# First q phase: the last column tile of q reads inputs with their shift already added

## The chip, the cores and the metric

One core of one Trainium2 chip. The metric is the device time of one execution in microseconds (us), median of several runs. The granted clock of the tensor engine was 1.00.

A ratio of two kernels is the mean time of one kernel's fast runs over the mean of the other's fast runs of the same rounds, so it is not quite the ratio of the medians quoted beside it.

Engines: PE is the tensor engine, PEld its weight loads, DVE the vector engine, ACT the scalar engine, POOL the third elementwise engine, SP the engine that issues DMA. A "tile" of x is 128 tokens, a "chunk" four tiles (512 tokens), a "k-tile" 128 of the 1024 features of a chunk. The "warm-up" is the matmuls at the kernel's start whose results nobody uses; a "pair" is one weight load with its matmul. A DMA "lands" when its data have arrived. "Lost time" is time that PE stands still where it could have run on.

## The reference, cut to what matters

```python
mod = (_silu(c) @ w_mod).reshape(c.shape[0], 6, 1, -1)
sa, ca, ga, sb, cb, gb = ...                       # six rows of 1024
h = _layernorm(x) * (1 + ca) + sa                  # x is 2048 x 1024
qkv = h @ wqkv                                     # q: the first 1024 columns
phi = lambda t: jnp.where(t > 0, t + 1, jnp.exp(t)) + 1e-06
pq, pk = phi(q), phi(k)
# ... linear attention, output projection, second norm, SwiGLU: not touched here
```

The shift `sa` is known later than the scale `1 + ca`, because its weights are loaded later. The kernel therefore starts q on inputs that are scaled but not shifted, and adds what is missing as a bias: q = Wq^T (scaled) + Wq^T sa.

## The kernel before

`P.pe`, `P.dve`, `P.act`, `P.pool` append an instruction to an engine's list; semaphores are worked out from the addresses that instructions touch. For PSUM this helper's unit is a whole bank: an access by another engine waits for the last one of this bank. HT[:, 0] holds the first chunk, transposed, in eight k-tiles dt; MODCOL holds the scale and shift columns.

```python
def h0_shift(dt):       # adds the shift to a scaled k-tile, in place
    P.dve("tensor_scalar", out=HT[:, 0, dt, :], in0=HT[:, 0, dt, :], scalar1=MODCOL[:, 1, dt:dt + 1],
          scalar2=None, op0=ALU.add)

def bias_mm(dts):       # column nt of bank 0 += Wq[dt, nt]^T sa[dt]: a matmul of one column
    for nt in range(NDT):
        for dt in dts:
            P.pe("matmul", out=PS[:, 0, 16 + nt:17 + nt], lhsT=WQK[:, dt, nt * 128:(nt + 1) * 128],
                 rhs=MODTMP[:, dt:dt + 1], start=False, stop=(dt == 3), skip_group_check=True)

def bias_fin():
    P.dve("tensor_copy", out=BIASQ[:], in_=PS[:, 0, 16:24])

def q_phase_chunk0(side):
    # [cut: q column tiles 0..6 over k-tiles 0..5; the scale columns; k-tiles 6, 7 get scale and shift at once]
    mod_sc(WSA, 0, range(4, 6))          # PE: sa for k-tiles 4, 5
    fin_sa(4, 2, True)                   # DVE: copy it to MODTMP and MODCOL
    for nt in range(7):
        if nt == 2:
            bias_mm((4, 5))
        q_part(nt, qb[nt], (6,))
    for nt in range(7):
        if nt == 1:
            mod_sc(WSA, 0, range(4))     # PE: sa for k-tiles 0..3
            fin_sa(0, 4, True)
            ln_ops[1][0]()               # DVE: statistics of tile 5 (second chunk), two halves
            ln_ops[1][1]()
        if nt == 4:
            bias_mm(range(4))
            bias_fin()
        q_part(nt, qb[nt], (7,))
    ln_ops[1][2]()
    ln1_rstd1(5)                         # DVE, then POOL: 1/std of tile 5
    for f in act_mv_ops(4):
        f()
    neg_rstd(4)                          # DVE, then POOL: 1/std of tile 4
    q_phi = lambda nt: phi_evac(..., bias=BIASQ[:, nt:nt + 1])
    for i, dt in enumerate((4, 5, 0, 1, 2, 3, 6, 7)):       # q column tile 7, in bank 0
        P.pe("matmul", out=PS[:, 0, :], lhsT=WQK[:, dt, 896:1024], rhs=HT[:, 0, dt, :], start=(i == 0),
             stop=(i == 7))
    for dt in (4, 5):
        h0_shift(dt)                     # k of this chunk needs shifted tiles
    ln1_xn(5); th_dma(5)                 # DVE: normalize tile 5; SP: its DMA transpose
    for dt in range(4):
        h0_shift(dt)
    ln1_xn(4); th_dma(4)
    for nt in range(8):
        q_phi(nt)                        # ACT and DVE: evacuate q
        # side work: statistics, normalization and transposes of tiles 6 and 7
# then k of chunk 0 (8 groups of 8 matmuls), in which DVE scales and shifts chunk 1,
# then k and q of chunk 1, ... and the G products (x^T times k), which read "pk" tiles
```

## Time and profile before

| | before |
|---|---|
| median of 6 runs | 831.10 us (830.88 to 831.48) |
| span of the profiled run | 829.0 us |
| PE busy | 819.6 us, 99% |
| last matmuls of the bias products | 26.33 to 27.11 us |
| last transpose of the second chunk lands | 41.80 us |
| 16 KB instruction fetch between 30 and 60 us | at 38.54 us, 1.03 us long |

First the page of the kernel before: busy time of each engine, and the engines of the chain that ended last.

```profile
PE 819.6 (99%) x4005; PEld 379.2 (46%) x4083; DVE 312.5 (38%) x665; ACT 197.5 (24%) x336; POOL 40.4 (5%) x57
...
PE 97%; DVE 2%; issue 1%; ACT 0%; DVEq 0%; ACTq 0%
```

PE is the limit. Only work that PE does, or that PE waits for, can count.

The PE timeline of the kernel before, from the sa matmuls on. Columns: start in us, length, engine, line, operation, out<-in, shapes, count.

```profile
20.55 0.54 PE L176 MATMUL ps<-siluc,wsa 128*128 128x1 bf16 x16
...
23.18 0.55 PE L176 MATMUL ps<-modtmp,wqk 128*128 128x1 bf16 x16
23.59 1.46 PE L176 MATMUL ps<-ht,wqk 128*128 128x512 bf16 x6
...
26.33 0.94 PE L176 MATMUL ps<-modtmp,wqk 128*128 128x1 bf16 x32
27.13 23.04 PE L176 MATMUL ps<-ht,wqk 128*128 128x512 bf16 x104
```

The lines that read `modtmp` are the 48 bias products. The 32 of them run from 26.33 to the next line's start, 27.13: 0.80 us, 25 ns each. A length such as 0.94 includes the modelled end of the last one, so starts are what to subtract. After 27.13 there is not one gap.

The DVE timeline of the kernel before, in the same stretch; brackets tell how long the engine sat idle and who ended that.

```profile
25.93 0.16 DVE L176 CAST modtmp<-ps 128x4 bf16<-128x4 f32 x1 [2.81 <-PE ps L176]
26.00 0.15 DVE L176 COPY modcol<-ps 128x4 f32<-128x4 f32 x1
26.22 1.29 DVE L176 BATCH_NORM_STATS2 stats<-xres 128x6 f32<-128x512 bf16 x2
27.42 0.15 DVE L176 COPY biasq<-ps 128x8 f32<-128x8 f32 x1
...
28.23 0.61 DVE L176 TENSOR_SCALAR ht<-ht,modcol 128x512 bf16<-128x512 bf16 x2
28.75 0.54 DVE L176 TENSOR_SCALAR xres<-xres,mv,rstd 128x1024 bf16<-128x1024 bf16 x1
29.21 1.13 DVE L176 TENSOR_SCALAR ht<-ht,modcol 128x512 bf16<-128x512 bf16 x4
30.26 0.54 DVE L176 TENSOR_SCALAR xres<-xres,mv,rstd 128x1024 bf16<-128x1024 bf16 x1
...
35.92 0.99 DVE L176 TENSOR_SCALAR xres<-xres,mv,rstd 128x1024 bf16<-128x1024 bf16 x2
...
41.93 2.67 DVE L176 TENSOR_SCALAR ht<-ht,modcol 128x512 bf16<-128x512 bf16 x8 [1.25 <-DMA ht<-xres]
```

Six shifts at 28.23 and 29.21, four normalizations at 28.75, 30.26 and 35.92 (`xres<-xres,mv,rstd`), and at 41.93 the scaling of the second chunk, which waits for its DMA transposes.

The PEld timeline of the kernel before at that place: the first k group of the second chunk.

```profile
42.89 1.61 PEld L176 LDWEIGHTS ps<-ht,wqk 128*128 128x128 bf16 x8
44.65 0.92 PEld L176 LDWEIGHTS ps<-ht,wqk 128*128 128x128 bf16 x5 [0.16 <-DVE ht L176]
```

One weight load, at 44.65, waits for DVE. PE loses nothing yet, but it is close.

Stretches of the kernel before around the instruction fetch. Columns: stretch, its length, busy time of PE, PEld, DVE, ACT, POOL with counts, clock, DMA share, GB/s.

```profile
38.30:38.60 0.30, 0.30 (x3) 0.13 (x2) 0.30 (x2) 0.30 (x2) 0.00 (x0) 1.00 1.33 259
...
39.20:40.20 1.00, 1.00 (x6) 0.49 (x5) 1.00 (x5) 1.00 (x3) 0.00 (x0) 1.00 0.61 10
40.20:41.00 0.80, 0.80 (x6) 0.35 (x4) 0.48 (x2) 0.80 (x2) 0.00 (x0) 1.00 1.09 217
```

The last column falls to 10 GB/s for a microsecond, in the middle of the transposes that DVE waits for. The trace's packet records show what is there: one packet of 16,384 bytes in the instruction queue from 38.54 to 39.57 us, and the transposes' packets of 256 bytes thinning out after it. The run has 32 such packets for PE's 4083 weight loads and as many matmuls; so I take them for PE's instruction fetches.

### The profile page before, as it was taken

What the parts mean: (1) busy time and instruction counts of PE and PEld (TensorE: products, weight loads), DVE (VectorE), ACT (ScalarE), POOL (GpSimd) and SP (SyncE); (2) the same over time, 40 slices, a digit from 0 to 9 for tenths busy, and PEclk for the clock granted to TensorE, in tenths of its full rate; (3) what the DMA queues carried; (4) which work ended last, traced back from release to release, by engine and by line L of the source; (5) the groups of instructions that cost most, each with busy time, mean ns of one, the idle gap of its engine ahead of it and who ended that gap; (6) DMA issues with size and microseconds to landing.
All of it is one profiled execution on the core that took longest, in us unless ns stands there. A gap on an engine that the chain in (4) does not pass through costs nothing.

```text
span 829.0 us, 9939 instructions
## 1 busy us (share of the span) xinstructions
PE 819.6 (99%) x4005; PEld 379.2 (46%) x4083; DVE 312.5 (38%) x665; ACT 197.5 (24%) x336; POOL 40.4 (5%) x57
## 2 busy tenths in 40 slices
PE   8999999999999999999999999999999999999998
PEld 4544444454444444444444444444444444444444
DVE  5797986756955521121221112122111111221111
ACT  4757641323242111011111101111110111111011
POOL 1010000000130000030000003000000300000000
PEclk9999999999999999999999999999999999999999
DMA  9969655928397995700455571045557004553000
GB/s 320 291 151 232 149 155 172 202 103 304 63 255 231 292 252 153 189 25 18 123 153 154 150 184 33 18 124 153 154 150 189 26 19 123 152 154 86 0 26 26
DMA packets 199245, 119.28 MB, mean 144 GB/s; under 512 B 57880, under 2 KB 182944, under 8 KB 199200
## 3 DMA queue, kind: packets, MB, share of 16 engines
q1 hardware_dynamic: 199184, 118.65, 52.8%
q8 instruction: 32, 0.52, 0.3%
q14 instruction: 13, 0.11, 0.0%
q10 hardware_dynamic: 16, 0.00, 0.0%
HBM read 100.67 MB, written 4.33 MB: 127 GB/s over the span
## 4 chain that ended last, share of the span: by engine, by line
PE 97%; DVE 2%; issue 1%; ACT 0%; DVEq 0%; ACTq 0%
PE ps L176 97%; DVE acc L176 1%; DVE pkt L176 0%; DVE e L176 0%; DVE pqt L176 0%; DVE ht L176 0%; DVE mask L176 0%; ACT e L176 0%; DVE xres L176 0%; DVE zsel L176 0%; DVE modcol L176 0%; DVEq L247 0%; ACTq L247 0%
## 5 line engine op out<-in xcount | busy, mean ns | idle before, releaser
L176 PE MATMUL ps<-h2t,guu 128*128 128x512 bf16 x878 | 210.1, 379 | 0.9
L176 PE MATMUL ps<-h2t,gug 128*128 128x512 bf16 x878 | 209.9, 379 | 0.9
L176 DVE TENSOR_TENSOR at<-sg,ps 128x512 bf16<-128x512 bf16 x112 | 77.0, 688 | 282.7 <-PE ps L176 270.1
L176 ACT ACTIVATE sg<-ps 128x512 bf16<-128x512 f32 x112 | 67.0, 598 | 309.6 <-PE ps L176 298.2
L176 PEld LDWEIGHTS ps<-h2t,guu 128*128 128x128 bf16 x896 | 87.7, 98 | 105.7
L176 PEld LDWEIGHTS ps<-h2t,gug 128*128 128x128 bf16 x896 | 87.6, 98 | 105.5
L176 PE MATMUL ps<-wd_a,at 128*128 128x512 bf16 (+1 forms) x501 | 111.5, 377 | 0.5
L176 PE MATMUL ps<-ht,wqk 128*128 128x512 bf16 x499 | 110.5, 379 | 0.8
L176 PE MATMUL ps<-wd_b,at 128*128 128x512 bf16 (+1 forms) x378 | 84.7, 377 | 0.4
L176 PEld LDWEIGHTS ps<-wd_a,at 128*128 128x128 bf16 x512 | 50.1, 98 | 59.7
L176 DVE TENSOR_TENSOR ut<-att,gb_b 128x512 bf16<-128x512 bf16 (+1 forms) x32 | 14.3, 446 | 166.9 <-ACT att L176 166.9
L176 PEld LDWEIGHTS ps<-ht,wqk 128*128 128x128 bf16 x512 | 49.5, 98 | 58.6 <-DVE biasq L176 0.2
L176 ACT ACTIVATE att<-ps 128x512 bf16<-128x512 f32 (+1 forms) x32 | 17.4, 591 | 182.1 <-PE ps L176 182.1
L176 PEld LDWEIGHTS ps<-wd_b,at 128*128 128x128 bf16 x384 | 37.6, 98 | 44.6
L176 PE MATMUL ps<-pk,xres 128*128 128x512 bf16 x250 | 55.9, 379 | 0.4 <-issue 0.2
L176 PE MATMUL ps<-mw,pqt 128*128 128x512 bf16 x250 | 55.8, 379 | 0.3
L176 POOL TENSOR_SCALAR h2t<-h2t,modcol 128x512 bf16<-128x512 bf16 x32 | 26.5, 844 | 383.0 <-DMA h2t<-xn 383.0
L176 ACT ACTIVATE e<-ps 128x512 bf16<-128x512 f32 x56 | 33.2, 604 | 31.7 <-PE ps L176 20.4
L176 PEld LDWEIGHTS ps<-mw,pqt 128*128 128x128 bf16 x256 | 24.8, 98 | 30.2 <-DVE xres L176 0.4
L176 PEld LDWEIGHTS ps<-pk,xres 128*128 128x128 bf16 x256 | 24.9, 98 | 29.9 <-issue 0.4
L176 ACT ACTIVATE junk<-xres 128x1024 bf16<-128x1024 bf16 x24 | 25.4, 1058 | 35.1 <-DVE xres L176 34.9
L176 DVE SCALAR_TENSOR_TENSOR xres<-ps,xres 128x512 bf16<-128x512 f32 x32 | 21.4, 688 | 12.3 <-PE ps L176 11.5
(107 smaller groups left out, 346.3 us busy)
## 6 DMA issues: line engine op xcount, KB each, us to landing
gug<-in_B_w_gate_dram SPq DMA_DIRECT2D x56, 512.0 KB, 4.1
guu<-in_B_w_up_dram SPq DMA_DIRECT2D x56, 512.0 KB, 5.3
xres<-in_A_x_dram SPq DMA_DIRECT2D x20, 256.0 KB, 7.8
rb<-recip_den SPq DMA_DIRECT2D x8, 512.0 KB, 12.0
stgx<-in_w_mod_dram SPq DMA_DIRECT2D x2, 2048.0 KB, 8.2
wd_a<-in_B_w_down_dram SPq DMA_DIRECT2D x4, 1024.0 KB, 7.8
out_dram<-xres SPq DMA_DIRECT2D x31, 128.0 KB, 1.7
xres<-in_A_x_dram SPq DMA_DIRECT2D x3, 1024.0 KB, 14.2
```

The source lines that it names most:

```text
L176: return getattr(e, method)(**kw)
```

## The change

Its intent: the eighth column tile of q is not begun before the shift is known. If it reads shifted inputs it needs no bias, and six one-column products fall away (two for k-tiles 4 and 5, four for 0 to 3). For that the six shifts move up to where `sa` becomes known, and the statistics of tile 5 move behind the bias copy.

```diff
         def bias_mm(dts):
-            for nt in range(NDT):
+            for nt in range(NDT - 1):
...
-            P.dve("tensor_copy", out=BIASQ[:], in_=PS[:, 0, 16:24])
+            P.dve("tensor_copy", out=BIASQ[:, 0:NDT - 1], in_=PS[:, 0, 16:23])
...
             fin_sa(4, 2, True)
+            for dt in (4, 5):
+                h0_shift(dt)
...
                     fin_sa(0, 4, True)
-                    ln_ops[1][0]()
-                    ln_ops[1][1]()
+                    for dt in range(4):
+                        h0_shift(dt)
...
-            ln_ops[1][2]()
+            for f in ln_ops[1]:
+                f()
...
-            q_phi = lambda nt: phi_evac(..., bias=BIASQ[:, nt:nt + 1])
-            for i, dt in enumerate((4, 5, 0, 1, 2, 3, 6, 7)):
+            q_phi = lambda nt: phi_evac(..., bias=BIASQ[:, nt:nt + 1] if nt < 7 else 0.0)
+            for i, dt in enumerate((6, 7, 4, 5, 0, 1, 2, 3)):
...
-            for dt in (4, 5):
-                h0_shift(dt)
             ln1_xn(5)
             th_dma(5)
-            for dt in range(4):
-                h0_shift(dt)
             ln1_xn(4)
```

More of the change, by code (lines that the diff above doesn't have):

```diff
@@ L784, in q_phase_chunk0 @@
             neg_rstd(4)
-            q_phi = lambda nt: phi_evac(qb[nt] if nt < 7 else 0, PQT[:, nt, 0:512], bias=BIASQ[:, nt:nt + 1])
-            for i, dt in enumerate((4, 5, 0, 1, 2, 3, 6, 7)):
+            q_phi = lambda nt: phi_evac(qb[nt] if nt < 7 else 0, PQT[:, nt, 0:512],
+                                        bias=BIASQ[:, nt:nt + 1] if nt < 7 else 0.0)
+            for i, dt in enumerate((6, 7, 4, 5, 0, 1, 2, 3)):
                 P.pe("matmul", out=PS[:, 0, :], lhsT=WQK[:, dt, 896:1024], rhs=HT[:, 0, dt, :], start=(i == 0),
                      stop=(i == 7))
-            for dt in (4, 5):
-                h0_shift(dt)
             ln1_xn(5)
             th_dma(5)
-            for dt in range(4):
-                h0_shift(dt)
             ln1_xn(4)
```

## The prediction

> **What bounds the kernel now.** The tensor engine: the page gives PE 819.6 of 829.0 us (99%) at a granted clock of 1.00, and the chain that ended last is 97% PE. The change touches only the first q phase (23 to 30 us in) and what its DVE order sends downstream.
>
> **Removed.** Six bias products (two of 16, four of 32), each a weight load and a one-column matmul. The timeline starts them 25 ns apart (26.33 to 27.11 us), as the Trainium skill, "TensorE: Matmul & The Clock Gate", section "Wait — 56ns, not 53.3ns?", says: never below about 25 ns however few columns. So 0.15 us less PE, where PE has no gaps and is on the chain.
>
> **Moved.** On DVE the six shifts (0.26 us apart) come right after their MODCOL copy. Two fall into idle DVE time at 23.1 us; four run from 26.15 to 27.25 us, just before the BIASQ copy, which waits for the bias products until about 27.27 anyway. So the last q group should find its bank and tiles ready, with a margin of about 0.05 us.
>
> The statistics of tile 5 (two of 0.61 us) now come after that copy: they end at about 28.7 instead of 27.5 us, and POOL's two powers (0.59 and 0.78 us, at 28.02 and 28.55) follow about 1.2 us later. In before shifts hid them; now nothing does. I estimate that the second normalization (tile 4) starts 0.2 to 0.4 us later than 30.26 us. DVE then works without gaps until 40.6 us, so normalizing tiles 6 and 7 (35.92, 36.38) is as much later, and so are their transposes.
>
> **Why it matters.** The second chunk's transposes land last at 41.80 us, DVE scales eight tiles from 41.93 to 44.60, and the last weight load of the next k group waits for them (44.653, 0.04 us late, no matmul lost). That place has about 0.05 us of slack: PE arriving 0.15 us earlier gives 0.10 back if the landing stays, and each further delay of it is a loss.
>
> A 16 KB instruction fetch at 38.54 us took 1.03 us, and the transposes' packets nearly stop from 39.3 to 40.3 us. The Trainium skill, "Runtime: NRT & Kernel Launch", section "Instruction fetch mechanics", has refills of 256 instructions; the trace agrees, one each 27 us (127 weight-load/matmul pairs). Twelve fewer PE instructions put that fetch about 1.1 us later, into the last transpose. Depending on where it falls the last landing is 41.3 to 42.3 us.
>
> **Sum.** -0.15 us removed, +0.10 for the exhausted slack, +0.15 (-0.1 to +0.5) for later transposes: about +0.1 us, far inside 2%.
>
> Predicted: 831.2 us, 80% range 830.6 to 831.9. Faster by over 2%: 0.01; within 2%: 0.98; slower by over 2%: 0.01.
>
> **What would show it.** Right: 42 instead of 48 products from MODTMP; the first k group about 0.15 us earlier; no PE gap before the last q group; normalizations of tiles 6 and 7 0.2 to 0.4 us later; a PE gap of 0.1 to 0.5 us near 44.5 us. Wrong: a PE gap near 27.5 us (BIASQ late), or none at 44.5 us (then up to 0.15 us faster).
>
> **What would make it wrong.** Shifts slower beside ACT, the fetch falling elsewhere, transposes held up by a full queue, or differences between runs (830.88 to 831.48) larger than the effect.

## The result, and the profile after

| | before | changed |
|---|---|---|
| median of 6 runs | 831.10 us (830.88 to 831.48) | 831.28 us (830.88 to 831.66) |
| span of the profiled run | 829.0 us | 829.3 us |
| first sa matmul | 20.55 us | 20.81 us |
| from there to the first G matmul | 105.70 us | 105.78 us |
| from the first G matmul to the end of the span | 702.74 us | 702.72 us |

The ratio of fast runs is 1.0002, 95% interval 0.9989 to 1.0015: the same, and an interval of about 1 us each way, much wider than what the change does. So the times alone settle nothing here. The profile can be cut finer. Nothing was changed ahead of the first sa matmul, and it starts anywhere from 20.55 to 21.72 us in the 14 profiles; that is scatter ahead of the change. Therefore the rest of this document counts from a point behind the start: the **stretch** from the first sa matmul to the first G matmul (the first that reads `pk`), or from the last bias product on.

The page of the changed kernel:

```profile
PE 824.0 (99%) x4077; PEld 378.1 (46%) x4077; DVE 312.1 (38%) x665; ACT 197.3 (24%) x336; POOL 40.2 (5%) x57
...
PE 98%; DVE 1%; DMA 0%; SPq 0%; issue 0%
```

PE shows more busy time here although it does less: 4077 matmuls are recorded against 4005, since some records were missing in the first trace. The weight loads, 4083 and 4077, show the six that went. Busy time cannot be compared at this size.

The PE timeline of the changed kernel:

```profile
20.81 0.54 PE L176 MATMUL ps<-siluc,wsa 128*128 128x1 bf16 x16
...
23.43 0.50 PE L176 MATMUL ps<-modtmp,wqk 128*128 128x1 bf16 x14
23.79 1.46 PE L176 MATMUL ps<-ht,wqk 128*128 128x512 bf16 x6
...
26.53 0.84 PE L176 MATMUL ps<-modtmp,wqk 128*128 128x1 bf16 x28
27.23 23.05 PE L176 MATMUL ps<-ht,wqk 128*128 128x512 bf16 x105
```

14 and 28 products instead of 16 and 32. From the first to the last product start it is 3.78 us instead of 3.93: 0.15 us saved. On the trace's clock 27.23 is later than 27.13, but 0.25 us of that is the later start.

The DVE timeline of the changed kernel:

```profile
23.41 0.61 DVE L176 TENSOR_SCALAR ht<-ht,modcol 128x512 bf16<-128x512 bf16 x2
26.13 0.16 DVE L176 CAST modtmp<-ps 128x4 bf16<-128x4 f32 x1 [2.11 <-PE ps L176]
...
26.39 1.14 DVE L176 TENSOR_SCALAR ht<-ht,modcol 128x512 bf16<-128x512 bf16 x4
27.45 0.16 DVE L176 COPY biasq<-ps 128x7 f32<-128x7 f32 x1
27.52 1.28 DVE L176 BATCH_NORM_STATS2 stats<-xres 128x6 f32<-128x512 bf16 x2
...
29.91 1.16 DVE L176 TENSOR_SCALAR xres<-xres,mv,rstd 128x1024 bf16<-128x1024 bf16 x2 [0.30 <-POOL rstd L176]
...
42.42 2.67 DVE L176 TENSOR_SCALAR ht<-ht,modcol 128x512 bf16<-128x512 bf16 x8 [1.46 <-DMA ht<-xres]
```

The shifts are early and the bias copy is in time for the last q group. DVE now waits for POOL at 29.91, as foreseen. The scaling of the second chunk starts at 42.42 instead of 41.93: 0.49 later, of which 0.25 is the start.

The PEld timeline of the changed kernel at the first k group of the second chunk:

```profile
42.77 1.18 PEld L176 LDWEIGHTS ps<-ht,wqk 128*128 128x128 bf16 x6
44.18 0.10 PEld L176 LDWEIGHTS ps<-ht,wqk 128*128 128x128 bf16 x1 [0.23 <-DVE ht L176]
44.50 0.10 PEld L176 LDWEIGHTS ps<-ht,wqk 128*128 128x128 bf16 x1 [0.23 <-DVE ht L176]
44.82 0.10 PEld L176 LDWEIGHTS ps<-ht,wqk 128*128 128x128 bf16 x1 [0.23 <-DVE ht L176]
45.15 0.55 PEld L176 LDWEIGHTS ps<-ht,wqk 128*128 128x128 bf16 x4 [0.23 <-DVE ht L176]
```

Weight loads come 0.32 us apart, which is DVE's pace for one k-tile, instead of PE's 0.216. The matmuls lose 0.23 us in all. That is more than the 0.15 us saved: the stretch is 0.08 us longer.

Stretches of the changed kernel around its fetch, in the columns given above:

```profile
39.00:39.40 0.40, 0.40 (x4) 0.18 (x2) 0.40 (x2) 0.40 (x2) 0.00 (x0) 1.00 0.75 141
...
40.00:41.10 1.10, 1.10 (x7) 0.51 (x6) 0.96 (x4) 1.10 (x3) 0.00 (x0) 1.00 0.53 13
41.10:41.70 0.60, 0.60 (x5) 0.24 (x4) 0.00 (x0) 0.57 (x3) 0.00 (x0) 1.00 1.16 267
```

The hole is there too, 0.9 us later (the fetch is at 39.46 us). From the packet records, the number of the transposes' 256-byte packets that start in each 0.2 us (from 38.34 us on before, from 38.26 changed):

```
us        38.3 38.5 38.7 38.9 39.1 39.3 39.5 39.7 39.9 40.1 40.3 40.5 40.7 40.9 41.1 41.3 41.5
before     158  147  129   86   26    0    6    8    7   16  217  226  156  226  108    0    0
changed    175  162  163  140  121  106  173  151   71   15    5    7    7    7   60  224  215
```

### The profile page after: what moved, and what is told of

Same layout as the page of the kernel before. It is cut to its first block, busy times and chain, and to the rows that moved or that the text cites. A ratio compares the mean times of both kernels' runs of the same rounds, so it can differ in the third digit from the quotient of the medians.

```text
span 829.3 us, 10006 instructions
## 1 busy us (share of the span) xinstructions
PE 824.0 (99%) x4077; PEld 378.1 (46%) x4077; DVE 312.1 (38%) x665; ACT 197.3 (24%) x336; POOL 40.2 (5%) x57
## 4 chain that ended last, share of the span: by engine, by line
PE 98%; DVE 1%; DMA 0%; SPq 0%; issue 0%
PE ps L176 98%; DMA xres<-in_A_x_dram 0%; DVE stats L176 0%; SPq L176 0%; DVE xres L176 0%; DVE ve L176 0%; DVE mv L176 0%; DVE nmr L176 0%
```

## The experiments

The theory: PE's saving is given back at the second chunk's first k group, where PE waits for DVE, DVE for the last transpose, and the landing of that transpose is set by where a PE instruction fetch falls; twelve PE instructions fewer move the fetch. Rivals: the later DVE work alone moves the landing; or the saving is kept and all else is start scatter.

Runs with rounds were timed three rounds against the kernel before on the same chip. All of them are the same as the kernel before at 2%. The last table of this section collects what the traces showed. They come from more than one chip: e, f2, g and d2 ran on one, a to d, i, j and the two repeats on another, and the chip of the first pair is not on record.

### a_products_only: the removal without the reordering

```diff
 # kernel before, with
-            for nt in range(NDT):                   # bias_mm
+            for nt in range(NDT - 1):
...
-            P.dve("tensor_copy", out=BIASQ[:], in_=PS[:, 0, 16:24])
+            P.dve("tensor_copy", out=BIASQ[:, 0:NDT - 1], in_=PS[:, 0, 16:23])
...
-            q_phi = lambda nt: phi_evac(..., bias=BIASQ[:, nt:nt + 1])
+            q_phi = lambda nt: phi_evac(..., bias=BIASQ[:, nt:nt + 1] if nt < 7 else 0.0)
 # column tile 7 still reads unshifted inputs, so its bias is missing: wrong on purpose
```

> The kernel before without the six bias products of the last q tile, in the old DVE order (that tile then lacks its bias, wrong on purpose). Stretch from the first matmul on the sa weights to the first G matmul: before 105.70 us, after 105.78. My theory (0.15 us is saved, and the slack of 0.05 us at the second chunk's first k group gives most of it back): tiles 6 and 7 normalized as in before (35.9, 36.4 us, less start jitter), the fetch about 1.1 us later than 38.5, last landing between 41.3 and 42.3 us, PE lost time at 43 to 46 us between 0 and 0.5 us, by where the fetch falls; stretch 105.55 to 106.0. Rival (saved time is simply kept and the +0.2 us was start jitter): no lost PE time there, stretch 105.55. Time within 0.4 us of before either way.

Measured: 831.44 us against 831.77 (ratio 0.9995, interval 0.998 to 1.001). Stretch 105.64: 0.15 us saved, 0.09 given back at the same place. The last landing was 21.35 us after the first sa matmul (before 21.25), the fetch at 18.51 (before 17.99). The rival (nothing given back) is out: the old DVE order loses too. Less was given back here than in the changed kernel, with an earlier fetch (18.51 against 18.65) and an earlier landing (21.35 against 21.49).

### b_order_only: the reordering without the removal

```diff
 # changed kernel, with
-            for nt in range(NDT - 1):
+            for nt in range(NDT):
...
-            P.dve("tensor_copy", out=BIASQ[:, 0:NDT - 1], in_=PS[:, 0, 16:23])
+            P.dve("tensor_copy", out=BIASQ[:], in_=PS[:, 0, 16:24])
```

> The changed kernel with all 48 bias products (the result is right, six products are computed in vain): only the DVE order and the tile's reading of shifted inputs differ from before. Theory: PE not earlier; tiles 6 and 7 normalized 0.25 to 0.3 us later than in before; fetch near 38.5 us as before; last landing 0.2 to 0.4 us later; PE lost time at 43 to 46 us 0.15 to 0.4 us, stretch 105.85 to 106.1 (before 105.70), time 0.1 to 0.4 us over before. Rival (DVE order is off the critical path): stretch 105.70, no lost time.

Measured: 831.32 us against 831.77 (0.9994, 0.998 to 1.0009). Stretch 105.72, lost time 0.02 us, not 0.15 to 0.4. My expectation missed: tile 7 was normalized at 15.95 us after the first sa matmul, against 15.82 in the kernel before (15.92 in its second profile), so the order costs at most 0.13 us, and PE had more slack than I thought. The last landing was 0.18 us later than in the kernel before (21.43 against 21.25), with the fetch 0.13 us later (18.12 against 17.99): that used up the slack, and no more. The reordering alone costs almost no time.

### c_no_products: take away seven times as much

```diff
 # changed kernel, without the calls of bias_mm; BIASQ copied from sa columns (wrong on purpose),
 # ahead of the four late shifts, and
-        warm(13, bank=3)                                # 13 matmuls of 512 columns in the start
+        warm(13, bank=3, split=13)                      # the same columns, each cut in four of 128
-        warm(5, bank=3)
+        warm(5, bank=3, split=1)                        # so 42 more weight-load/matmul pairs
```

> The changed kernel with none of the 42 remaining products (q's bias columns are filled with other values, wrong on purpose), so PE loses 1.05 us of products and about 0.09 us of a wait on DVE; 42 extra pairs in the warm-up (same columns in all, cut in narrower matmuls) keep the PE instruction count before the q phase's end. Theory: the transposes land as in the changed kernel, so PE only waits longer: lost time at 43 to 46 us 1.0 to 1.6 us, stretch within 0.35 us of 105.78, time within 0.5 us of the changed kernel. Rival (PE work here is on the critical path and saved work is kept): stretch 104.6 to 104.7, time 1.1 us less.

Measured: 831.46 us against 831.77 (0.9995, 0.9979 to 1.0012): an interval that leaves room for a gain of 1.05 us (0.9987) and for none, so the trace has to tell. The stretch is 105.38, 0.40 less than in the changed kernel, just outside the 0.35 that I gave, and far from the rival's 104.6 to 104.7. With no wait it would have been 105.55 - 1.05 - 0.09 = 104.41, so 0.97 us came back as waits. My second miss: only 0.38 us of it at the second chunk, since the last landing was not as in the changed kernel but 0.40 us earlier (21.09 us after the first sa matmul against 21.49). The rest is in two earlier places. The PE timeline of this run has the larger one, a wait for ACT:

```profile
26.51 3.18 PE L176 MATMUL ps<-ht,wqk 128*128 128x512 bf16 x14
29.98 20.39 PE L176 MATMUL ps<-ht,wqk 128*128 128x512 bf16 x92 [0.29 <-ACT rl L176]
```

The first k group needs the PSUM bank that ACT evacuates; the start at 29.98 is 0.67 us after the previous one instead of 0.22, a loss of 0.45 us. A further 0.15 us is lost before the last sa matmuls, at 25.70, whose weights a DMA had not yet brought. So more than one wait stands behind PE in this phase.

### d_fetch_moved: move the fetch by 54 pairs

```diff
 # changed kernel, with
+        warm(13, bank=3, split=13)
+        warm(5, bank=3, split=5)
```

> The changed kernel with 54 more weight-load/matmul pairs in the warm-up (18 matmuls of 512 columns cut in four; same columns in all), which should move every 16 KB PE instruction fetch about 11.6 us earlier in the q and k phases: 39.5 to about 28, and none between 33 and 42 us. Theory: tiles 6 and 7 normalized as in the changed kernel (36.2, 36.6 us), but last landing at about 41.3 instead of 42.3 us, no PE lost time at 43 to 46 us (under 0.05), stretch 105.55, so 0.2 us better than the changed kernel and 0.15 better than before; time 0.1 to 0.3 us less than the changed kernel, hardly visible. Rival (the later landing is due to the later DVE work alone, and the fetch does nothing): last landing 42.0 or later, lost time 0.1 us or more.

Measured: 832.53 us against 831.77 (1.0021, 0.9996 to 1.0047). One of its four runs took 836.77 (at a mean granted clock of 0.998), as no other did. In the place in question theory held: the fetch was gone (12.24 us after the first sa matmul, 6.4 us earlier and not 11.6 as I had expected), the last landing was 20.39 us instead of 21.49, with tiles normalized at the same time, and no matmul was lost between 43 and 46 us. The hole was gone too: from the third transpose's first packet to the fourth's last, at least 116 start in each 0.2 us, but for the first and the last of these. The rival, for which the fetch does nothing, is out. But the trace as a whole is longer, which I had not expected (the times alone, with 1 inside the interval, do not show it): PE lost 0.08 us at 114.6, 0.68 at 118.7 and 0.68 at 147.4 us. A later fetch had moved to 110.08 us and took 1.70 us there. First the DVE line of this run, then the same line of the kernel before:

```profile
112.74 0.75 DVE L176 TENSOR_SCALAR acc<-stg,siluf 128x1024 f32<-128x1024 bf16 x1 [3.76 <-DMA stg<-in_w_mod_dram]
```

```profile
110.52 0.75 DVE L176 TENSOR_SCALAR acc<-stg,siluf 128x1024 f32<-128x1024 bf16 x1 [1.87 <-DMA stg<-in_w_mod_dram]
```

DVE waited 1.9 us longer for a 2 MB load. PE then waited for DVE to free a bank. That a fetch also slows this load is my reading of these two lines and of the fetch's place; the next run supports it.

### d2_fetch_moved_less: move it by 30 pairs

```diff
 # changed kernel, with
+        warm(13, bank=3, split=10)
```

> The changed kernel with 30 instead of 54 more pairs in the warm-up, so that fetches in the k and q phases come about 6.5 us earlier: 39.2 to about 33 to 35 us, 94.4 to about 88, 121.5 to about 115, none within the big weight load at 102 to 112 us into which the earlier try had moved one. Theory: last landing 20.4 to 20.8 us after the first sa matmul, no lost time at 43 to 46 us, none at 114 to 119 and 147 us; stretch 105.55 (0.15 better than before), time about 0.2 us less than the changed kernel. Rival (the losses of the earlier try come from the warm-up itself): losses at 114 to 119 and 147 us again.

Measured: 831.19 us against 831.20 (1.0001, 0.9986 to 1.0016). Stretch 105.55, last landing 20.76 us after the first sa matmul, nothing lost at 43 to 46 or at 114 to 119 us; 0.04 us at 146.0. So the losses of the run before came from where the fetch fell, not from a cut warm-up as such. One miss: the fetch came only 2.6 us earlier than in the changed kernel (at 37.13 us), not about 6.5. Here PE's saving is kept whole: 0.15 us less than before in the stretch.

### e_stats_early: another DVE order

```diff
 # changed kernel, with
                     fin_sa(0, 4, True)
-                    for dt in range(4):
-                        h0_shift(dt)
+                    ln_ops[1][0]()              # moved up; the later lines that had these are taken out
+                    ln_ops[1][1]()
...
                     bias_fin()
+                    ln_ops[1][2]()
+                    ln1_rstd1(5)
+                    for dt in range(4):
+                        h0_shift(dt)
...
             th_dma(5)
+            ln_ops[2][0]()          # first half of tile 6's statistics, taken from later
             ln1_xn(4)
```

> The changed kernel with another DVE order: the statistics of tile 5 go back in front of the bias copy, the four late shifts come after it (the last q group reads those tiles last), and the first half of tile 6's statistics fills the wait for POOL. Counted from the first sa matmul: tile 7 normalized at 15.4 to 15.6 us (before 15.83, changed 15.84), last landing at 20.9 to 21.3 us with the fetch where it is (before 21.25, changed 21.49). Theory: PE arrives 0.15 us earlier and finds its tiles: lost time at 43 to 46 us under 0.08 us, stretch from the first sa matmul to the first G matmul 105.55 to 105.63 (before 105.70, changed 105.78). Rival (the landing follows the fetch, not DVE): landing 21.4 or later, lost time 0.15 us or more. Time at most 0.25 us better than before, hardly visible.

Measured: 831.11 us against 831.20 (1.0000, 0.9985 to 1.0015). The rival was right. Tiles were normalized even earlier than I expected (tile 7 at 15.12 us after the first sa matmul, 0.72 before the changed kernel), yet the last landing was later, 21.80, and PE lost 0.54 us, more than in the changed kernel. SP issued the third transpose at 16.00 us, though its tile was ready before: the issue of the second one took until then. And the fetch fell at 18.96. Earlier DVE work does not bring the landing forward when the queue and the fetch hold it.

### f2_both: the other DVE order, and the fetch moved by 30 pairs

```diff
 # e_stats_early, with
+        warm(13, bank=3, split=10)
```

> The other DVE order and the fetch moved by 30 pairs together. Theory: once PE finds its tiles there is nothing more to gain in this place: stretch 105.55, as with either alone, and last landing 20.0 to 20.5 us after the first sa matmul, the earliest of all. Rival (each is worth something of its own beyond the wait): stretch below 105.5.

Measured: 830.95 us against 831.20 (0.9998, 0.9982 to 1.0015). Stretch 105.55, as with the fetch moved alone; last landing 20.43 us. Once PE finds its tiles, an earlier landing is worth nothing. By the stretch this run and d2_fetch_moved_less beat both kernels by 0.15 us or more; by the time no such difference can be told apart.

### g_stats_twice: double the work that was moved

```diff
 # changed kernel, with
-            for f in ln_ops[1]:
+            for f in ln_ops[1][:2] + ln_ops[1]:
```

> The changed kernel with tile 5's two statistics instructions done twice (1.2 us more DVE after the bias copy; the result stays right). Theory: tiles 6 and 7 are normalized and sent 1.2 us later (tile 7 at 17.05 us after the first sa matmul), the last landing is 0.5 to 1.2 us later than 21.49, PE loses 0.7 to 1.5 us at 43 to 46 us (0.23 in the changed kernel), stretch 106.25 to 107.0, time 0.5 to 1.2 us over the changed kernel. Rival (DVE in this stretch is off the critical path): stretch 105.8, same time.

Measured: 832.33 us against 831.20 (1.0014, interval 1.0000 to 1.0029). Stretch 107.14, lost time 1.58 us (a little over the expected range), last landing 22.85. So DVE work ahead of the normalizations is on PE's path when there is enough of it: 1.2 us more of it cost 1.36 us of stretch. The real reordering delays it by only 0.0 to 0.2 us. One thing I had not foreseen: the fetch came 1.1 us later too (19.78 us after the first sa matmul against 18.65), with the same PE instructions. So their number is not all that places a fetch, and the later landing here is not due to DVE alone. The whole first k group waited, as the waits of PEld between 40 and 48 us show (in total, times, longest):

```profile
PEld ps L176 <- DVE ht L176: 2.7, 8, 1.1
```

### i_fetch_back and j_fetch_back_more: give the twelve instructions back

These two and the next two are single runs.

```diff
 # changed kernel, with
+        warm(13, bank=3, split=2)      # i: 6 more pairs, as many PE instructions as before
+        warm(13, bank=3, split=4)      # j: 12 more pairs
```

> All times here are counted from the first sa matmul. So far the PE time lost at the second chunk (the stretch less 105.55 us, or less 105.70 with all 48 products) has been the last landing less 21.26 us (less 21.41 with 48 products) in every run, whatever the DVE order. This kernel is the changed one with 6 more pairs in the warm-up, as many PE instructions as the change took away. Theory (the twelve missing instructions move the fetch and the fetch moves the landing): fetch at about 18.0 (before 17.99, changed 18.65), last landing 21.1 to 21.4, lost time 0 to 0.12 us (changed 0.23), stretch 105.55 to 105.67. Rival (the landing differs by chance or by DVE order): fetch and landing as in the changed kernel, 18.5 to 18.7 and 21.4 to 21.5, stretch 105.7 to 105.8.

Measured: 830.97 us; the kernel before on this chip 831.27. The fetch is back at 17.88 us after the first sa matmul (before 17.99, changed 18.65), the last landing at 21.19 (21.25, 21.49), lost time 0, stretch 105.55. The waits of PEld between 40 and 48 us read as those of the kernel before:

```profile
PEld ps L176 <- DVE ht L176: 0.2, 1, 0.2
```

This is the run that decides, though it is a single profile; j, d2 and d, which move the fetch by more, agree with it. The instructions added do no useful work and stand far ahead, yet they take away the whole loss.

> The changed kernel with 12 more pairs in the warm-up. Theory: fetch 0.5 to 1.3 us earlier than in the changed kernel (17.3 to 18.1 us after the first sa matmul), last landing 20.8 to 21.25, no lost time, stretch 105.55. Rival: as in the changed kernel, stretch 105.7 to 105.8.

Measured: 831.14 us. Fetch at 17.08, a little earlier than the 17.3 to 18.1 that I gave, last landing 21.12, nothing lost at the second chunk. The stretch was 105.65, 0.10 over what I expected: PE waited 0.09 us for DMA of the sa weights before the last bias products, which is ahead of everything here. Counted from the last product it is 99.145, as it should be.

### r_changed_again and r_before_again: the scatter of profiles

No edit.

> The changed kernel once more, unaltered, for the scatter between profiles. Theory: fetch 18.4 to 18.9, last landing 21.3 to 21.7, stretch 105.6 to 106.0, and lost time equal to landing less 21.26 to within 0.03 us. Rival (the 0.23 us was a single event): stretch 105.55.

Measured: 831.68 us. Fetch 18.89, last landing 21.63, lost time 0.39 us, stretch 105.94. The loss was no single event. The lost time is the landing less 21.26 within 0.02 us.

> The kernel before once more, unaltered. Theory: fetch 17.8 to 18.3, last landing 21.1 to 21.45, stretch 105.70 to 105.75. Rival (scatter of the landing is as large as the difference between the kernels): landing 21.5 or later, stretch over 105.8.

Measured: 831.72 us. Fetch 17.96, last landing 21.24, nothing lost at the second chunk; stretch 105.75, of which 0.05 us again lie before the last bias product.

### All traces together

Times counted from the last bias product (us). "Lost" is the time from there to the first G matmul less 99.145, the value of every trace in which nothing was lost, of both kernels. Tile 7, issue, fetch and landing come from the trace's records of instructions, packets and landings. c_no_products has no bias product to count from and is left out.

| kernel | bias products | extra pairs | tile 7 normalized | last issue | fetch | last landing | lost |
|---|---|---|---|---|---|---|---|
| before | 48 | 0 | 9.27 | 10.65 | 11.43 | 14.69 | 0.00 |
| r_before_again | 48 | 0 | 9.32 | 10.70 | 11.35 | 14.63 | 0.00 |
| b_order_only | 48 | 0 | 9.40 | 10.78 | 11.56 | 14.87 | 0.02 |
| changed | 42 | 0 | 9.44 | 10.82 | 12.25 | 15.08 | 0.23 |
| r_changed_again | 42 | 0 | 9.44 | 10.82 | 12.48 | 15.23 | 0.39 |
| a_products_only | 42 | 0 | 9.24 | 10.63 | 12.11 | 14.94 | 0.09 |
| e_stats_early | 42 | 0 | 8.71 | 10.95 | 12.55 | 15.39 | 0.54 |
| g_stats_twice | 42 | 0 | 10.62 | 12.00 | 13.36 | 16.43 | 1.58 |
| i_fetch_back | 42 | 6 | 9.44 | 10.82 | 11.48 | 14.79 | 0.00 |
| j_fetch_back_more | 42 | 12 | 9.43 | 10.82 | 10.58 | 14.62 | 0.00 |
| d2_fetch_moved_less | 42 | 30 | 9.43 | 11.19 | 9.66 | 14.36 | 0.00 |
| f2_both | 42 | 30 | 8.69 | 10.07 | 9.98 | 14.03 | 0.00 |
| d_fetch_moved | 42 | 54 | 9.44 | 10.82 | 5.83 | 13.99 | 0.00 there, 0.78 later |

Two things are to be read from it. The loss is the last landing less 14.85 us, or nothing, in all 13 traces, within 0.01 us (14.85 is fitted to them; the slope of one is not); so at this place PE in the kernel before had a margin of 14.85 - 14.69 = 0.16 us. And in eight of the traces the landing follows the fetch, at one of two distances. Fetches at 12.11, 12.25, 12.48, 12.55 give landings at 14.94, 15.08, 15.23, 15.39, always 2.75 to 2.84 us on, though tile 7 was normalized anywhere from 8.71 to 9.44. In the four runs with as many PE instructions as the kernel before, fetches at 11.35, 11.43, 11.48, 11.56 give 14.63, 14.69, 14.79, 14.87, 3.26 to 3.31 us on. Why the two distances differ is not shown. In g_stats_twice, with all its transposes later, it is 3.07 us.

## Why the prediction was right

**What is removed: right, to the hundredth.** 0.15 us predicted, 3.93 - 3.78 = 0.15 us measured between first and last product.

**The last q group finds its bank and tiles: right.** PE starts its matmuls 0.215 to 0.217 us apart from 27.23 us on in the changed kernel, with the bias copy at 27.45.

**"I estimate that the second normalization (tile 4) starts 0.2 to 0.4 us later", and tiles 6 and 7 with it: wrong in size, and the trace's own clock hides it.** It shows 36.65 after 36.38, just what I forecast. But the changed kernel's run started its phase 0.25 us later. Counted from the first sa matmul tile 7 is normalized at 15.84 against 15.82 (in the second profiles 15.84 against 15.92). The reordering by itself does delay it, by 0.19 us between a_products_only and the changed kernel, and by 0.03 to 0.13 between the two profiles of the kernel before and b_order_only. The removal brings the bias copy, and DVE behind it, forward by about as much; which of the waits around POOL I had taken as too long was not looked into.

**The margin at the second chunk: "about 0.05 us" was too small.** It was 0.16 us: a weight load that waits can still be followed by its matmul at once. That is why b_order_only lost only 0.02 us.

**The fetch: right in kind, too large in size.** I said 1.1 us later; it was 0.66 and 0.93 us later in the two pairs of profiles (17.99 to 18.65, 17.96 to 18.89 us after the first sa matmul). Giving the twelve instructions back undid it (i_fetch_back). I had taken PE's full pace, one fetch each 27 us; that is the median, but the fetch before this one lay only 9.8 us ahead of it (28.74 us in the kernel before). What sets the place besides the number of instructions stays open (see g_stats_twice).

**The sum: right, partly because errors cancelled.** Predicted -0.15 + 0.10 + 0.15 = +0.10 us. In the traces it is -0.15 + 0.23 = +0.08 us, and for the second pair, counted from the last bias product, -0.15 + 0.39 = +0.24 us. In the prediction's own terms, for the first pair: the exhausted slack cost about nothing instead of 0.10 (0.15 us earlier against a margin of 0.16), and the landing, 0.24 us later after the first sa matmul (21.25 to 21.49), cost 0.23 instead of 0.15. That it was later came mostly through the fetch and little through DVE: with the fetch given back and DVE's order kept (i_fetch_back) the landing is at 14.79 us after the last product, 0.10 later than in the kernel before, against 0.39 in the changed kernel. The predicted gap of 0.1 to 0.5 us near 44.5 us was there. The median, 831.28 us, is beside the predicted 831.2 us, but times that scatter by 0.6 us from run to run cannot confirm a tenth; so near a hit is luck.

What stays open: how the fetch stops the transposes. The records show one packet of 16 KB that takes about a microsecond and the transposes' packets failing at the same time; they do not tell on which of the 16 DMA engines a packet ran. That one engine is held up and the rest wait for it is my inference. Nor is it shown why the landing differs by 0.15 us between the two profiles of the changed kernel, other than that the fetch differs too, by 0.23 us.

## What to carry to other kernels

A saving on the limiting engine is worth only as much as the margin of the next thing which that engine waits for: find that wait downstream and read its margin before counting the gain. When differences are a few tenths of a microsecond, subtract from a landmark in the same trace that lies behind the start scatter; the trace's own clock and the total time both mislead. And count instructions too: in this kernel removing or adding a few on PE moved its instruction fetches, and a fetch that fell into a DMA which somebody waited for cost more (0.23 and 0.39 us) than the instructions had (0.15 us).

## What the Trainium skill lacked or had wrong

- "Runtime: NRT & Kernel Launch", section "Instruction fetch mechanics": it says that refills come in 16 KiB blocks of 256 instructions and that crossing a boundary is "mostly hidden". The traces agree with the size (packets of 16,384 bytes, with a median of 27 us between them, some 127 weight-load/matmul pairs). It lacks that a fetch of 0.88 to 1.03 us, at the same time as DMA transposes, brought their 256-byte packets from over 150 to 16 or fewer in each 0.2 us for about a microsecond, and that such a fetch, where it came 0.66 and 0.93 us later than before, cost PE 0.23 and 0.39 us in the two profiles of the changed kernel.
- The same section lacks that the place of a fetch can be chosen: 6, 12 and 30 pairs more in the start moved it from 12.25 to 11.48, 10.58 and 9.66 us after the last bias product. The shift is not 0.216 us for each pair: here it is 0.77 us for 6 pairs, 1.67 for 12 and 2.59 for 30.
- "TensorE: Matmul & The Clock Gate", section "Wait — 56ns, not 53.3ns?": the floor of about 25 ns from start to start held for one-column matmuls, each with its weight load: 25 ns. Nothing to mend.
- No page that I found gives a number for how late a waiting weight load may come without a loss. Here, where each weight load waited for DVE, its matmul started 4 ns later (45.146 and 45.150 us), while a free-running one was 0.21 us ahead of its matmul.
